# One transformer block on one core: the last 512 queries of attention in two jobs of 256, PSUM banks from one pool

## The chip, the core and the metric

One core of a Trainium2 chip runs the kernel. The metric is device time in microseconds (us), the median of several executions without a profiler. The profile pages come from one more execution with the hardware profiler on; its times are its own and are named as such. Engines in the profile: PE is TensorE (matmul), PEld its weight loads, DVE is VectorE, ACT is ScalarE, POOL is GpSimd, SP is SyncE, which issues the DMAs.

## The reference

One pre-norm transformer block on 2048 tokens of width 1024, in bf16. The attention has 32 heads of 32 columns, no mask. The feed-forward part (FFN) has 3584 hidden columns and a tanh GELU.

```
h  = x + softmax((ln(x) wq) (ln(x) wk)^T * 32**-0.5) (ln(x) wv) wo     # per head, heads joined
h2 = h + gelu(ln(h) w1 + b1) w2 + b2
```

The kernel gets `A_x`, `A_wqkv`, `A_wo`, `B_w1`, `B_b1`, `B_w2`, `B_b2` and writes `h2`.

## The kernel before

**A planner writes the order.** The kernel's Python describes every instruction as a `Task` with an engine, a cost in us, the buffers it reads and writes, a priority and a kind. `Graph.schedule` (L98) plays the tasks through by these costs and fixes the order of each engine's queue; `assign` adds the semaphore waits and `emit` writes the queues out. On the chip each engine then runs its queue strictly in that order, however long things take there. The costs are constants: a 512-column matmul pack 0.2225 us (`MM` and 0.003), an exp of 1024 columns 0.953 us (`c_act`), DMA 280 GB/s and 2.1 us latency, 0.1 us for a change of TensorE's tiling.

**What TensorE does next** is `pick_pe` (L913): a ready QK task always; else a PV task if five are waiting (`PV_FORCE`), if no background is ready, or after the last QK; else the oldest ready background task ("bg"). ScalarE, VectorE and SyncE take the ready task of lowest priority number, then the oldest.

**Attention.** The queries are cut in four chunks of 512. A head pair `p16` (16 of them) is worked on at a time; `g` is a group of two pairs, 128 columns. One round (`attention_round`, L687, `Att.qk`, L619) is one QK task: four matmuls with 32-row tiling at once, two key tiles of 128 by two heads, into four PSUM banks (L634). Two exp instructions on ScalarE follow (L643), each 128x1024 from two banks into a slot of the ring `PT`. There are three such two-bank units, banks 0 to 5. A PV task (`pv_unit`, L647) adds one key tile: two matmuls with V (L654) and two with a matrix of ones (L658), each on 32 columns of the array, all at once, into bank 6. A pair has 8 rounds, 16 exps and 16 PV tasks; then `finish` (L665) copies sums and outputs out of bank 6 on VectorE (L666, L668), and after the second pair of a group takes reciprocals (L673) and multiplies into `OT` (L680; in the very last group by quarters, L677). `load_q` fetches the group's queries from DRAM.

**Background.** While chunk `qc` is in attention, the work of chunk `qc - 1` runs between its rounds, in bank 7 alone: `wo` (L703, output projection, 8 accumulations of 8 matmuls, evicted into `hch` by L719), `ln2` (L723, layer norm per tile of 128 tokens on VectorE and GpSimd, eight transposes, L508, and their eviction into `hnT`, L512 or L514), `ffn1` (L735, 28 accumulations of 8, eviction with bias L748, then square, L754, scalar_tensor_tensor, L756, Tanh on ScalarE, L758, and L760 into `gT`) and `ffn2` (L763, for each half `j` of the output columns and each of four token tiles one bias matmul and 28 matmuls, evicted by L782). In the background every 128x128 by 512 matmul is issued as four matmuls on 32 columns each (`narrow`, L439), so that TensorE need not change its tiling between background and PV. Weights come in 512 KB tiles: `w1r` has four buffers, `w2r` seven. In the chunks before the last, `late_q` also projects later queries.

**Tail.** After the last attention, chunk 3's `wo`, `ln2`, `ffn1` and `ffn2` run alone, with full 128x128 matmuls (L443), eight banks in turn, buffers `R2` laid over the keys and values, and evictions of `ln2` and `ffn1` on ScalarE (L512, L751).

Of the kernel before, what the change touches and what calls it, by code (L numbers as in the profile page):

```python
# [27 lines left out]
class Task:  # L28
    __slots__ = ("eng", "fns", "occ", "lat", "deps", "prio", "kind", "mode", "left", "succ", "ready", "done",
                 "order", "inc", "flow", "value", "lane", "waits", "bytes", "hold")  # L30

    def __init__(self, eng, fns, occ, lat, prio, kind, mode):
        self.eng, self.fns, self.occ, self.lat = eng, fns, occ, lat
        self.prio, self.kind, self.mode = prio, kind, mode
        self.deps = set()
        self.succ = []
        self.left = 0
        self.ready = 0.0
        self.done = None
        self.order = None  # L40
        self.inc = False
        self.flow = None
        self.value = 0
        self.lane = None
        self.waits = ()
        self.bytes = 0
        self.hold = None


class Graph:  # L50
# [7 lines left out]
    def __init__(self, n_lanes):  # L58
        self.tasks = []
        self.regions = {}  # L60
        self.n_lanes = n_lanes

# [35 lines left out]
    def schedule(self, pick_pe, switch=0.1, dma_rate=280.0, dma_lat=2.1, dma_issue=0.06):  # L98
# [13 lines left out]

        def release(t):
            t.ready = max([d.done - (d.lat if d.eng == t.eng == E.PE else 0.0) for d in t.deps], default=0.0)
            heapq.heappush(upcoming[t.eng], (t.ready, num[t], t))
            heapq.heappush(events, t.ready)
# [5 lines left out]
        while n < total:  # L122
# [5 lines left out]
            for e in self.ENGS:  # L128
                while free[e] <= now + 1e-9:
# [18 lines left out]
                    rd.remove(t)  # L148
                    start = now
                    if e == E.PE:  # L150
# [19 lines left out]
                    heapq.heappush(events, free[e])  # L170
                    n += 1
# [113 lines left out]
def build_kernel(nc, A_x, A_wqkv, A_wo, B_w1, B_b1, B_w2, B_b2, out):  # L285
# [143 lines left out]
    def pe(fns, occ, reads=(), writes=(), kind="bg", mode="full", prio=0, after=()):  # L429
        return gr.add(E.PE, fns, occ, 0.16, reads, writes, prio, kind, mode, after)  # L430

    def mm(bank, lhsT, rhs, start, stop, reads, narrow, cols=(0, 512)):
# [3 lines left out]
        if narrow:  # L436
            fns = []
            for j in range(4):
                fns.append(lambda p, j=j: p.matmul(psum[32 * j:32 * j + 32, bank, c0:c1], lhsT[:, 32 * j:32 * j + 32], rhs,  # L439
                                                   start=start, stop=stop, tile_position=(0, 32 * j), skip_group_check=True))  # L440
            pe(fns, occ, reads=reads, writes=[B_ps[bank]], mode="col")
        else:
            pe(lambda p: p.matmul(psum[:, bank, c0:c1], lhsT, rhs, start=start, stop=stop),  # L443
               occ, reads=reads, writes=[B_ps[bank]], mode="full")
# [61 lines left out]
    def transposes(src_ap, B_src, bank, dst_ap, B_dst, evac, prio):  # L506
        for dc in range(DC):
            pe(lambda p, dc=dc: p.transpose(psb[:, bank, dc * P:(dc + 1) * P], src_ap[:, dc * P:(dc + 1) * P], ident[:]),  # L508
               0.064, reads=[B_src, B_ident], writes=[B_ps[bank]], prio=prio)
        src = psb[:, bank, :].rearrange("p (dc t) -> p dc t", dc=DC)  # L510
        if evac == "act":
            act(lambda a: a.activation(dst_ap, src, ACT.Copy), 1024, reads=[B_ps[bank]], writes=[B_dst], prio=-1)  # L512
        else:
            dve(lambda v: v.tensor_copy(dst_ap, src), c_dve_ps(1024), reads=[B_ps[bank]], writes=[B_dst])  # L514

# [19 lines left out]
    def proj(which, g, tc, bank, evac, direct=False):  # L535

        blk, c = divmod(which * D + g * P, 512)
        for dc in range(DC):
            mm(bank, Wall[:, blk, dc, c:c + P], xnT[:, tc, dc, :], dc == 0, dc == DC - 1,
# [3 lines left out]
        if evac == "act":  # L543
            act(lambda a: a.activation(stg[:, s, :], psum[:, bank, :], ACT.Copy), 512,
                reads=[B_ps[bank]], writes=[B_stg[s]], prio=-1)
        else:
            dve(lambda v: v.tensor_copy(stg[:, s, :], psum[:, bank, :]), c_dve_ps(512), reads=[B_ps[bank]], writes=[B_stg[s]])  # L547
# [28 lines left out]
    def late_q(R, qc, gs):  # L576

        dma(R.xq[:, :, :], xd[qc - 1], P * 8192, reads=[B_xd[qc - 1]], writes=[R.B_xq], prio=0)
        for g2 in range(gs // 2, G // 2):
            s = wblock(R, A_wqkv[:, 256 * g2:256 * g2 + 256], 0)  # L580
            for k in range(2):
                g = 2 * g2 + k
                for dc in range(DC):
                    mm(7, R.w1[:, s, dc, k * P:k * P + P], R.xq[:, dc, :], dc == 0, dc == DC - 1,
                       [R.B_w1[s], R.B_xq], True)
                o = R.next("os", R.nos)
                dve(lambda v, o=o: v.tensor_copy(R.ost[:, o, :], psum[:, 7, :]), c_dve_ps(512),
                    reads=[B_ps[7]], writes=[R.B_ost[o]])
                dma(qd[g, qc], R.ost[:, o, :], P * 1024, reads=[R.B_ost[o]], writes=[B_qd[g][qc]], prio=0)

    def proj_v(tt, q, bank, evac):

        blk, c = divmod(256 * q, 512)
        blk += 4
        for k in range(2):
            tc, t4 = divmod(tt + k, 4)
            for dc in range(DC):
                mm(bank, xnT[:, tc, dc, t4 * P:(t4 + 1) * P], Wall[:, blk, dc, c:c + 256], dc == 0, dc == DC - 1,
                   B_W[blk][c // P:c // P + 2] + [B_xnTt[tc][t4]], True, cols=(256 * k, 256 * k + 256))
        dst = V[:, tt:tt + 2, 256 * q:256 * q + 256]  # L600
        src = psum[:, bank, :].rearrange("p (t c) -> p t c", t=2)
        wr = [B_V[4 * (tt + k) + q] for k in range(2)]
        if evac == "act":
            act(lambda a: a.activation(dst, src, ACT.Copy), 512, reads=[B_ps[bank]], writes=wr, prio=-1)
        else:
            dve(lambda v: v.tensor_copy(dst, src), c_dve_ps(512), reads=[B_ps[bank]], writes=wr)  # L606


    class Att:
# [9 lines left out]
        def qk(self, qc, units):  # L619

            fns, banks, rd, us = [], [], [], []
            for p16, kt in units:
                tc, k4 = divmod(kt, 4)
                half, i = divmod(k4, 2)
# [5 lines left out]
                for j in range(2):  # L630
                    r0 = 64 * half + 32 * j

                    def fn(p, j=j, r0=r0, u=u, p16=p16, tc=tc, i=i, qs=qs, pr=pr):
                        return p.matmul(psum[:, 2 * u + j, :], KT2[r0:r0 + 32, p16, tc, i, :],  # L634
                                        QT2[r0:r0 + 32, qs, pr, :], start=True, stop=True, tile_position=(r0, 0))
                    fns.append(fn)
                banks += [B_ps[2 * u], B_ps[2 * u + 1]]
                rd += [B_KT[4 * p16 + tc][half], B_QTh[qs][half][pr]]
            pe(fns, 0.224, reads=rd, writes=banks, kind="qk", mode="row")
            for (p16, kt), u in zip(units, us):  # L640
# [4 lines left out]
                self.pv.append((qc, p16, kt, s))  # L645

        def pv_unit(self, bank, first, last):  # L647
            qc, p16, kt, s = self.pv[self.done]
            self.done += 1
            g, pr = divmod(p16, 2)  # L650
            fns = []
            for j in range(2):
                h = 2 * p16 + j
                fns.append(lambda p, j=j, h=h: p.matmul(  # L654
                    psum[32 * j:32 * j + 32, bank, :], V[:, kt, 32 * h:32 * h + 32], PT[:, s, j, :],
                    start=first, stop=last, tile_position=(0, 32 * j), skip_group_check=True))
            for j in range(2):
                fns.append(lambda p, j=j: p.matmul(  # L658
                    psum[64 + 32 * j:96 + 32 * j, bank, :], ones32[:, :], PT[:, s, j, :],
                    start=first, stop=last, tile_position=(0, 64 + 32 * j), skip_group_check=True))  # L660
            pe(fns, 0.224, reads=[B_PT[s], B_V[4 * kt + (p16 // 4)], B_ones], writes=[B_ps[bank]], kind="pv", mode="col")
            if last:
                self.finish(qc, g, pr, bank)

        def finish(self, qc, g, pr, bank):  # L665
            dve(lambda v: v.tensor_copy(Dsb[64 * pr:64 * pr + 64, :], psum[64:128, bank, :]), c_dve_ps(512),  # L666
                reads=[B_ps[bank]], writes=B_Dsb[pr], prio=-1)
            dve(lambda v: v.tensor_copy(Osb[64 * pr:64 * pr + 64, :], psum[0:64, bank, :]), c_dve_ps(512),  # L668
                reads=[B_ps[bank]], writes=[B_Osb[pr]], prio=-1)
            self.fin.add((qc, g, pr))  # L670
            if (qc, g, 1 - pr) in self.fin:
                for k in range(4):
                    dve(lambda v, k=k: v.reciprocal(Dsb[:, 128 * k:128 * k + 128], Dsb[:, 128 * k:128 * k + 128]), 0.93,  # L673
                        reads=[B_Dsb[0][k], B_Dsb[1][k]], writes=[B_Dsb[0][k], B_Dsb[1][k]], prio=1)
                    if qc == NCH - 1 and g == G - 1:
                        c = slice(128 * k, 128 * k + 128)
                        dve(lambda v, c=c: v.tensor_tensor(OT[:, qc % 2, g, c], Osb[:, c], Dsb[:, c], ALU.mult), c_dve(128),  # L677
                            reads=[B_Dsb[0][k], B_Dsb[1][k]] + B_Osb, writes=[B_OT[qc % 2][g][k]], prio=1)
                if not (qc == NCH - 1 and g == G - 1):
                    dve(lambda v: v.tensor_tensor(OT[:, qc % 2, g, :], Osb[:, :], Dsb[:, :], ALU.mult), c_dve(512),  # L680
                        reads=B_Dsb[0] + B_Dsb[1] + B_Osb, writes=B_OT[qc % 2][g], prio=1)
# [5 lines left out]
    def attention_round(qc, p16, r):  # L687
        tc, i = divmod(r, 2)
        att.qk(qc, [(p16, 4 * tc + i), (p16, 4 * tc + 2 + i)])
        while len(att.pv) - att.done > PV_LAG:  # L690
            att.pv_unit(6, att.done % 16 == 0, att.done % 16 == 15)

    def attention_flush():
        while len(att.pv) > att.done:
            att.pv_unit(6, att.done % 16 == 0, att.done % 16 == 15)
# [7 lines left out]
    def wo(R, qc, banks, RX):  # L703
        nb = 0
# [3 lines left out]
        for t4 in range(4):  # L708
            for j in range(2):
                s = ws[2 * j]  # L710
                bank = banks[nb % len(banks)]
                nb += 1
                tt = qc * 4 + t4
                for k, g in enumerate([7, 0, 1, 2, 3, 4, 5, 6] if len(banks) == 1 else range(G)):
                    mm(bank, OT[:, qc % 2, g, t4 * P:(t4 + 1) * P], R.w1[:, s:s + 2, g, :], k == 0, k == 7,
                       [B_OT[qc % 2][g][t4], R.B_w1[s], R.B_w1[s + 1]], len(banks) == 1)
# [290 lines left out]
```

## Time and profile before

| | us |
|---|---|
| median of three executions | 1203.92 (1203.0 to 1205.25) |
| profiled execution, its span | 1417.9 |
| ScalarE, 1024 exps (L643) | 989.2 busy, 1.025 each |
| VectorE, all | 673.2 busy |
| L439 `a_w2r,gT`, FFN2 in the background, 2688 matmuls | 241.9 |
| L439 `a_hnT,a_w1r`, FFN1 in the background, 2688 matmuls | 215.2 |
| L443 `a_hnT,b_w1r` and `a_w2r,gT`, FFN1 and FFN2 of the tail | 64.5 and 64.1 |
| last exp ends, last matmul starts | 1255.0, 1413.4 |

How to read it: the profiled execution took 1417.9 us from first to last instruction, while the executions without profiler took 1203.92 us in the median, 0.849 of it. The page's row of TensorE clock shows 0.7 nearly everywhere (0.749 in the mean). The clock of the executions without profiler is not recorded. A group's busy time is the union of its instructions, from start to a modelled end, so groups that overlap on TensorE add up to more than the engine's own busy time.

### The profile page before, as it was taken

How to read it: one execution, taken by the hardware profiler on the slowest of the kernel's cores; microseconds unless marked ns; L12 is line 12 of the kernel's file. 1: busy time of each engine (PE TensorE's matmuls, PEld its weight loads, DVE VectorE, ACT ScalarE, POOL GpSimd, SP SyncE). 2: the span in 40 equal slices, each digit the busy share in tenths (PEclk: the TensorE clock that was granted, in tenths of full speed). 3: DMA queues.
4: the chain of work that ended last, by engine and by line, in shares of the span. 5: the costliest groups of instructions: out<-in, count | busy, mean ns of one | idle time of the engine just before them, and what ended most of it. 6: DMA issues, size and time to landing. Idle time of an engine off the chain costs nothing.

```text
span 1417.9 us, 37847 instructions
## 1 busy us (share of the span) xinstructions
PE 1366.2 (96%) x17326; PEld 510.9 (36%) x17336; DVE 673.2 (47%) x1165; ACT 1085.3 (77%) x1189; POOL 37.9 (3%) x96
## 2 busy tenths in 40 slices
PE   8999999999999999999999999999999999978999
PEld 5544443433333333332333333333333333324333
DVE  7354444443546774223547762225677612245710
ACT  4778787878888888888888888888988888844500
POOL 2000000000100000000100000000000000001000
PEclk7777777777777777777777777777777777766777
DMA  6800000025343222303342230422323322202222
GB/s 165 224 2 13 28 13 14 13 72 156 101 122 101 76 69 72 124 16 98 107 124 71 83 98 16 124 71 63 107 73 98 102 66 85 87 0 75 74 93 71
DMA packets 165793, 112.29 MB, mean 79 GB/s; under 512 B 25345, under 2 KB 162817, under 8 KB 164866
## 3 DMA queue, kind: packets, MB, share of 16 engines
q1 hardware_dynamic: 165634, 109.87, 26.2%
q8 instruction: 136, 2.23, 0.7%
q14 instruction: 23, 0.19, 0.1%
HBM read 98.58 MB, written 11.27 MB: 77 GB/s over the span
## 4 chain that ended last, share of the span: by engine, by line
PE 91%; ACT 4%; DVE 3%; issue 1%; POOL 1%; DMA 0%; POOLq 0%; DVEq 0%
PE ps L439 48%; PE ps L654 17%; PE ps L634 12%; PE ps L443 10%; ACT PT L643 3%; PE ps L658 2%; PE ps L798 1%; ACT xnT L512 1%; DVE a_xh L748 1%; PE ps L508 1%; DVE V L606 0%; DVE stg L547 0%; DVE Osb L668 0%; DVE Dsb L666 0%; DMA a_w1r<-in_A_wqkv_dram 0%
## 5 line engine op out<-in xcount | busy, mean ns | idle before, releaser
L643 ACT ACTIVATE PT<-ps 128x1024 bf16<-128x1024 f32 x1024 | 989.2, 1025 | 180.5 <-PE ps L634 166.1
L654 PE MATMUL ps<-PT,V 128*32 128x512 bf16 x2048 | 383.4, 457 | 13.7 <-DVE V L606 6.2
L658 PE MATMUL ps<-PT,ones 128*32 128x512 bf16 x2048 | 384.8, 458 | 0.0
L439 PE MATMUL ps<-a_w2r,gT 128*32 128x512 bf16 x2688 | 241.9, 452 | 0.0
L634 PE MATMUL ps<-QT,KT 32*128 32x512 bf16 x2048 | 216.7, 414 | 7.4 <-ACT PT L643 7.3
L439 PE MATMUL ps<-a_hnT,a_w1r 128*32 128x512 bf16 x2688 | 215.2, 454 | 4.0 <-DVE a_xh L748 3.2
L654 PEld LDWEIGHTS ps<-PT,V 128*32 128x32 bf16 x2048 | 103.3, 104 | 143.9 <-issue 89.3
L634 PEld LDWEIGHTS ps<-QT,KT 32*128 32x128 bf16 x2048 | 51.5, 91 | 272.3 <-ACT PT L643 164.5
L439 PE MATMUL ps<-xnT,Wall 128*32 128x512 bf16 x1344 | 111.6, 453 | 7.0 <-ACT xnT L512 4.8
L439 PEld LDWEIGHTS ps<-a_w2r,gT 128*32 128x32 bf16 x2688 | 77.3, 109 | 112.0 <-issue 103.3
L673 DVE RECIPROCAL Dsb<-Dsb 128x128 f32<-128x128 f32 x128 | 115.1, 928 | 1.0
L439 PEld LDWEIGHTS ps<-a_hnT,a_w1r 128*32 128x32 bf16 x2688 | 70.6, 107 | 108.0 <-issue 71.4
L782 DVE SCALAR_TENSOR_TENSOR a_ost<-ps,hch 128x512 bf16<-128x512 f32 x24 | 16.6, 692 | 189.8 <-PE ps L439 189.7
L658 PEld LDWEIGHTS ps<-PT,ones 128*32 128x32 bf16 x2048 | 103.5, 104 | 6.6 <-issue 6.6
L748 DVE TENSOR_SCALAR a_xh<-ps,b1f 128x512 bf16<-128x512 f32 x84 | 63.1, 751 | 81.3 <-PE ps L439 80.2
L666 DVE COPY Dsb<-ps 64x512 f32<-64x512 f32 x64 | 44.4, 694 | 101.5 <-PE ps L658 100.1
L439 PE MATMUL ps<-Wall,xnT 128*32 128x256 bf16 x2048 | 83.8, 314 | 0.0
L547 DVE CAST stg<-ps 128x512 bf16<-128x512 f32 x40 | 27.5, 689 | 89.2 <-PE ps L439 89.2
L443 PE MATMUL ps<-a_hnT,b_w1r 128*128 128x512 bf16 x219 | 64.5, 470 | 2.1 <-ACT a_hnT L512 1.5
L439 PEld LDWEIGHTS ps<-Wall,xnT 128*32 128x32 bf16 x2048 | 57.6, 107 | 22.7 <-issue 11.3
L443 PE MATMUL ps<-a_w2r,gT 128*128 128x512 bf16 x219 | 64.1, 461 | 0.5
L439 PE MATMUL ps<-a_w1r,OT 128*32 128x512 bf16 x768 | 63.1, 453 | 0.8 <-DVE hch L719 0.5
(69 smaller groups left out, 875.5 us busy)
## 6 DMA issues: line engine op xcount, KB each, us to landing
a_w2r<-in_B_w_dram SPq DMA_DIRECT2D x56, 512.0 KB, 4.6
a_w1r<-in_B_w_dram SPq DMA_DIRECT2D x42, 512.0 KB, 3.9
a_w1r<-in_A_wo_dram SPq DMA_DIRECT2D x16, 512.0 KB, 4.7
QT<-q_scratch SPq DMA_DIRECT2D x60, 128.0 KB, 2.8
b_w1r<-in_B_w_dram SPq DMA_DIRECT2D x14, 512.0 KB, 3.8
a_w1r<-in_A_wqkv_dram SPq DMA_DIRECT2D x11, 512.0 KB, 5.1
xrb<-in_A_x_dram SPq DMA_DIRECT2D x16, 256.0 KB, 3.9
Wall<-in_A_wqkv_dram SPq DMA_DIRECT2D x16, 256.0 KB, 5.4
```

What stands on the lines that cost most here:

```text
L439: fns.append(lambda p, j=j: p.matmul(psum[32 * j:32 * j + 32, bank, c0:c1], lhsT[:, 32 * j:32 * j + 32], rhs, start=start, stop=stop, tile ...
L443: pe(lambda p: p.matmul(psum[:, bank, c0:c1], lhsT, rhs, start=start, stop=stop), occ, reads=reads, writes=[B_ps[bank]], mode="full")
L508: pe(lambda p, dc=dc: p.transpose(psb[:, bank, dc * P:(dc + 1) * P], src_ap[:, dc * P:(dc + 1) * P], ident[:]), 0.064, reads=[B_src, B_ide ...
L547: dve(lambda v: v.tensor_copy(stg[:, s, :], psum[:, bank, :]), c_dve_ps(512), reads=[B_ps[bank]], writes=[B_stg[s]])
L634: return p.matmul(psum[:, 2 * u + j, :], KT2[r0:r0 + 32, p16, tc, i, :], QT2[r0:r0 + 32, qs, pr, :], start=True, stop=True, tile_position= ...
L643: act(lambda a, u=u, s=s: a.activation(PT[:, s, :, :], psum[:, 2 * u:2 * u + 2, :], ACT.Exp, bias=0.0, scale=SCALE), 1024, reads=[B_ps[2 * ...
L654: fns.append(lambda p, j=j, h=h: p.matmul(psum[32 * j:32 * j + 32, bank, :], V[:, kt, 32 * h:32 * h + 32], PT[:, s, j, :], start=first, st ...
L658: fns.append(lambda p, j=j: p.matmul(psum[64 + 32 * j:96 + 32 * j, bank, :], ones32[:, :], PT[:, s, j, :], start=first, stop=last, tile_po ...
L666: dve(lambda v: v.tensor_copy(Dsb[64 * pr:64 * pr + 64, :], psum[64:128, bank, :]), c_dve_ps(512), reads=[B_ps[bank]], writes=B_Dsb[pr], p ...
L673: dve(lambda v, k=k: v.reciprocal(Dsb[:, 128 * k:128 * k + 128], Dsb[:, 128 * k:128 * k + 128]), 0.93, reads=[B_Dsb[0][k], B_Dsb[1][k]], w ...
L748: dve(lambda v, i=i, fc=fc, bank=bank: v.tensor_scalar(R.xh[:, i, :], psum[:, bank, :], b1f[:, fc:fc + 1], None, ALU.add), c_dve_ps(512), ...
L782: dve(lambda v, o=o, t4=t4, j=j, bank=bank: v.scalar_tensor_tensor(R.ost[:, o, :], psum[:, bank, :], 0.5, hch[:, t4, 512 * j:512 * j + 512 ...
```

## The change

- The list `jobs` replaces the loop over chunks: chunks 0 to 2 as before, then chunk 3 as two jobs, queries 0 to 255 and 256 to 511, each over all heads and keys. Beside the first runs the background of chunk 2, beside the second that of the first half (two token tiles), and the tail holds the second half alone.
- In a job of 256 queries one QK task has eight matmuls of 256 columns: each bank takes two key tiles side by side. The exp instructions keep their size. A PV task has eight matmuls of 256 columns, for two key tiles. A pair has 4 rounds; `finish` copies 256 columns. Each of the two jobs loads the queries.
- `wo`, `ln2`, `ffn1` and `ffn2` take token tiles or columns. For 256 queries, `ffn1` puts two of its 28 column blocks into one bank (matmuls of 256 columns), evicts them separately and runs the GELU steps on both at once. Every weight is loaded once more, since five jobs load what four did.
- Accumulations of the background are groups, numbered in program order. The planner opens them strictly in that order and gives each a bank from a pool when its first matmul is picked; the bank returns when its readers are done. The pool holds bank 7 from the start of the main attention, and the other seven join after their last use by the attention.
- An eviction of `ffn1` or `ln2` has an alternative on ScalarE. Once all exps are planned, it goes to the engine that has less planned work waiting.

```diff
 def release(t):
+    if t.alt is not None and late():
+        e2, fns2, occ2, lat2 = t.alt
+        if load[e2] + occ2 < load[t.eng] + t.occ:
+            t.eng, t.fns, t.occ, t.lat = e2, fns2, occ2, lat2
+    load[t.eng] += t.occ
...
+                    if e == E.PE and t.grp is not None and t.grp.bank is None:
+                        x = min(banks(now))
+                        pool.remove(x)
+                        t.grp.bank = x[1]
+                        state["next"] += 1
...
-def qk(self, qc, units):
+def qk(self, qc, units, q0=0, nq=512):
+    nk = 512 // nq
...
-    return p.matmul(psum[:, 2 * u + j, :], KT2[r0:r0 + 32, p16, tc, i, :],
-                    QT2[r0:r0 + 32, qs, pr, :], start=True, stop=True, tile_position=(r0, 0))
+    return p.matmul(psum[:, 2 * u + j, nq * k:nq * k + nq], KT2[r0:r0 + 32, p16, tc, i, :],
+                    QT2[r0:r0 + 32, qs, pr, q0:q0 + nq], start=True, stop=True, tile_position=(r0, 0))
...
+            fns = [f for _, f in sorted(fns, key=lambda x: x[0])]
+            pe(fns, 0.224 if nk == 1 else 0.23, reads=rd, writes=banks, kind="qk", mode="row")
...
-def wo(R, qc, banks, RX):
+def wo(R, qc, RX, narrow, t4s=range(4)):
...
+                gp = gr.group()
...
+            for f in range(0, 2, nk):
+                fcs = [2 * blk + f + k for k in range(nk)]
+                gp = gr.group()
+                i = R.next("gl", R.ngl)
+                for k, fc in enumerate(fcs):
+                    fo = (fc % 2) * P
+                    for dc in range(DC):
+                        mm(gp, R.w1[:, s, dc, fo:fo + P], R.hnT[:, dc, cols], dc == 0, dc == DC - 1,
+                           [R.B_w1[s]] + hn, narrow, cols=(nq * k, nq * k + nq))
...
+    jobs = [(0, 0, 512), (1, 0, 512), (2, 0, 512), (3, 0, 256), (3, 256, 256)]
+    for n in range(1, len(jobs)):
+        qc, q0, nq = jobs[n - 1]
+        t4s = range(q0 // P, (q0 + nq) // P)
+        if n == 1:
             late_q(R1, 1, 2)
-        wo(R1, qc - 1, [7], R1)
-        ln2(R1, qc - 1, [7], (lambda qc=qc: late_q(R1, qc + 1, 0)) if qc + 1 < NCH else None)
-        ffn1(R1, qc - 1, [7])
-        ffn2(R1, qc - 1, [7])
-        attention_chunk(qc)
+        wo(R1, qc, R1, True, t4s)
+        ln2(R1, (lambda n=n: late_q(R1, n + 1, 0)) if n < 3 else None, t4s)
+        ffn1(R1, True, slice(q0, q0 + nq))
+        ffn2(R1, qc, True, t4s)
+        attention_chunk(*jobs[n])
         attention_flush()
...
+    for b in range(7):
+        gr.join(b, B_ps[b].w + B_ps[b].r)
...
+            if t.grp is not None and t.grp.bank is None and (not free or t.grp.n != state["next"]):
+                continue
```

## The prediction

> **What bounds the kernel now.** I read the page first: busy time by engine, the granted clock, the chain that ended last.
>
> ```profile
> span 1417.9 us, 37847 instructions
> PE 1366.2 (96%) x17326; PEld 510.9 (36%) x17336; DVE 673.2 (47%) x1165; ACT 1085.3 (77%) x1189; POOL 37.9 (3%) x96
> PEclk7777777777777777777777777777777777766777
> PE 91%; ACT 4%; DVE 3%; issue 1%; POOL 1%; DMA 0%; POOLq 0%; DVEq 0%
> ```
>
> TensorE is busy 96% of the span, is 91% of the chain, and runs at 0.75 of its clock. A change that only moves matmuls gains what TensorE idles now, no more. So I looked for its idle time around the last chunk: a table by stage. Columns: busy time of PE, PEld, DVE, ACT and POOL, each with its count, then clock, DMA share, GB/s.
>
> ```profile
> 960.00:1011.00 51.00, 46.86 (x592) 15.84 (x588) 30.47 (x51) 45.65 (x49) 6.21 (x16) 0.75 0.29 82
> 1011.00:1115.00 104.00, 102.52 (x1352) 35.64 (x1348) 75.47 (x124) 90.62 (x106) 0.00 (x0) 0.75 0.31 88
> 1115.00:1233.00 118.00, 117.75 (x1560) 39.62 (x1558) 33.46 (x47) 99.62 (x105) 0.00 (x0) 0.75 0.28 85
> 1233.00:1256.00 23.00, 18.92 (x164) 4.55 (x157) 2.66 (x4) 21.04 (x23) 0.00 (x0) 0.68 0.02 6
> 1256.00:1272.00 16.00, 15.37 (x57) 5.76 (x55) 11.66 (x20) 0.00 (x0) 0.00 (x0) 0.75 0.01 1
> 1272.00:1284.00 12.00, 3.96 (x32) 3.30 (x34) 6.86 (x19) 3.98 (x4) 6.38 (x16) 0.57 0.00 1
> 1284.00:1349.00 65.00, 64.34 (x220) 25.65 (x224) 45.46 (x80) 32.02 (x53) 0.00 (x0) 0.73 0.28 81
> 1349.00:1415.00 66.00, 65.44 (x228) 25.88 (x231) 7.61 (x12) 1.84 (x3) 0.00 (x0) 0.75 0.26 86
> ```
>
> The first three rows are the last chunk's attention with chunk 2's background beside it: output projection (wo) and layer norm (ln2), then FFN1, then FFN2. In FFN1 and FFN2 TensorE has 1.7 us free out of 222. Only after 1233 is there room (18.92 of 23). Then comes the tail alone: wo, a hole of 12 us while ln2 runs on VectorE and GpSimd, FFN1, FFN2.
>
> The timeline of TensorE fixes where the background ends:
>
> ```profile
> 1232.31 0.76 PE L439 MATMUL ps<-a_w2r,gT 128*32 128x512 bf16 x8
> 1245.02 0.39 PE L634 MATMUL ps<-QT,KT 32*128 32x512 bf16 x4 [0.50 <-ACT PT L643]
> 1246.85 0.42 PE L634 MATMUL ps<-QT,KT 32*128 32x512 bf16 x4 [0.47 <-ACT PT L643]
> ```
>
> Chunk 2's last FFN2 matmul starts before 1233. By the same view ten QK rounds follow (1233.27 to 1252.35). Without background a round lasts 1.83 us (1245.02 to 1246.85) and waits for ScalarE.
>
> **The change, part by part.** Units first. I call four narrow matmuls that start together, or one full one, a pack. FFN2 of the tail is 232 packs (224 and 8 of bias) in the 66 us from 1349 to 1415: 0.2845 us each. A round's own work is one QK and two PV packs, 0.85, plus two changes of tiling. The timeline shows 0.415 from a column pack to QK and 0.351 from QK back, against 0.2845: 0.20 together. So a round without background leaves 1.83 - 1.05 = 0.78 us, 2.7 packs.
>
> *Where the moved work lands.* The two jobs together have the same 128 rounds. Chunk 2's background keeps its place in TensorE's order and keeps its 520 packs, so it still ends some ten rounds before the end, now inside the second job. The first half's background (wo 32 packs, FFN1 112, FFN2 116) queues behind it, in strict order of groups. In ten rounds only its wo fits: chunk 2's wo took 31.2 us for 64 packs (965.8 to 997.0), so 32 take 15.6, from 1233 to about 1249. FFN1 and FFN2 of the first half therefore still run after the attention, as narrow packs, and the second half's wo, ln2, FFN1 and FFN2 behind them. So the change mostly cuts the tail in two rather than hiding it.
>
> *The tail before*, from the last PV pack at 1256.8: wo 14.5, hole 12.8 (to 1284.1), FFN1 64.5, FFN2 66.4, last eviction and store 2.9: 161.1.
>
> *The tail after*, term by term:
> - Hole until FFN1 of the first half. From the last wo pack to FFN1, chunk 2 took 14.2 (997.0 to 1011.2) for four tiles. Two tiles, ending at 1249, give between 7 and 14, so FFN1 starts at 1256 to 1263. Bounds 0 to 8; I take 4.
> - FFN1, 112 x 0.2845 = 31.9, as 224 packs of 256 columns. The V projection has such packs (groups by shape): 83.8 us for 512 of them, 0.164 each, against 0.142 for half a pack. But that busy time counts ends; start to start the timeline mostly shows 0.138. I take 0.142.
> - FFN2, 116 x 0.2845 = 33.0.
> - Waits for w2 tiles: seven buffers, now freed and refilled within one token tile's 8 us instead of three times that. Seven tiles at the fastest rate of the trace, 329 GB/s (1380 to 1385), take 11.2 us plus latency. Bounds 0 to 3 for each half; I take 1.5.
> - wo of the second half, 32 x 0.2845 = 9.1.
> - Second hole. At least the last tile's chain: 0.69 hch, 1.28 statistics, 0.2, about 2.2 on GpSimd, 0.55, 1.0 transposes, 1.0 eviction: 7. At most the 12.8 of today. I take 9.
> - Slow clock behind the holes: 0.73 instead of 0.75 over 65 us is 1.7 today. For two holes I take 2.7.
> - FFN1 31.9, FFN2 33.0, tile wait 1.5, end 2.9.
>
> Sum 160.5, against 161.1: nothing gained. Wo moved into the rounds pays for the second hole, and not more.
>
> *What is added in the attention.* Every head pair now hands over PSUM bank 6 twice per 512 queries, 16 handovers more. ScalarE waited for PV 12.9 us in all (waits), over 64 handovers: 0.2 each, 3.2 (bounds 0 and twice that). Wo beside the last rounds: 1.0. QK and PV of 256 columns double the instructions and weight loads; PV is nearest to the V projection's rows and costs nothing. QK packs back to back on the same rows occur nowhere. Bounds: 0, or a weight load of 0.091 uncovered in each of 128 rounds, 11.6. I take 0, since ScalarE sets many of those rounds. QT is loaded 16 times more (128 KB, 2.8 us), ahead of use and behind free slots; the 16.8 MB of weights loaded once more come at a mean of 79 GB/s today. Both nothing, unless SyncE's queue holds them back; that is in the tile waits.
>
> *Shared evictions.* The tail's ScalarE did 28 evictions and its FFN1 ran at PE 64.34 of 65, so moving some to VectorE, already busy 45.46, releases nothing. The pool is one bank during the attention, as before. Nothing for both; that cover goes if VectorE takes most evictions: 14 pairs x (1.8 + 0.8) is 36 us, 4 over the matmuls.
>
> Total: 161.1 becomes 160.5 + 4.2, so 1417.9 becomes **1421.5**. The profiled execution was slower than the three timed runs: 1203.92 / 1417.9 = 0.849. If all scales alike, 1207. If plain runs have the full clock, packs shrink by a quarter (35.8 us off the old tail, 34.7 off the new), while holes and waits stay and tile waits double (+3): -0.6 + 1.1 + 3.0 + 4.2 = +7.7, or 1211.6. The trace does not tell which; I take the middle, **1209**.
>
> A rule that speaks against the change: the Trainium skill, "TensorE: Matmul & The Clock Gate", section "What's actually happening", says that an idle window of about 3.4 us halves the array's clock, and knows only full and half clock. The trace has 0.75 for over a millisecond, so here the measurement decides, and it has 0.57 in the 12 us hole. By the page each hole costs about one window at half rate, an estimate of 1.7 us of work: 3.4 for two, 0.7 more than my term.
>
> **Rivals.**
> - *The second job has room after all (faster).* If chunk 2's background leaves more rounds to the first half, each hides 0.78 us of tail. For it: 0.78 us free per round without background. Against: TensorE busy 117.75 of 118 where the work would have to go. Eighteen rounds more give 18 x 0.78 x 0.849 = 12 us: **1197**. It decides from eleven rounds more (11 x 0.66 = 7.3, more than 5.1 and the 0.2%).
> - *Half packs cost (slower).* The uncovered QK weight load, 11.6, and narrow FFN1 at 0.164 instead of 0.142, 224 x 0.022 = 4.9: 16.5 x 0.849 = 14 more, **1223**. For it: no row shows QK packs back to back. Against: weight loads lie beside matmuls everywhere (PEld 36%).
> - *It doesn't do what it says:* the halves change nothing measurable. That is my forecast with smaller holes, and its share of "same".
>
> **How the numbers follow.** Forecast 0.56 (own range 1200 to 1217), faster rival 0.25, slower rival 0.19. Lowest bounds of all terms: 160.5 - 4 - 2 - 3 - 1, so -10.6 x 0.849 = 1195; highest: +10.9 for holes, waits and clock, 6 handovers, 1, 11.6: 29.5 x 0.849 = 1229. Beside the rivals, 8 in 10 is 1193 to 1225. About 0.2% (2.4 us) is what a measurement of this kernel can tell from no change. Faster: 0.25 + 0.04 = 0.29. Same: 0.17. Slower: 0.35 + 0.19 = 0.54.
>
> **What would show it.** Right: narrow FFN1 and FFN2 packs (256 columns in FFN1) after the last exp; two holes of 4 to 10 us with a low clock; chunk 2's last FFN2 pack about ten rounds before the last QK. Wrong: narrow FFN packs of the first half between QK rounds (room); rounds above 1.83 us without background (half packs); matmuls of FFN1 waiting for w1 tiles (transfers).

## The result and the profile after

The changed kernel takes **1208.93 us** (median of four, 1208.04 to 1210.17), the kernel before 1203.93 beside it: a ratio of 1.0043 [1.0028, 1.0057], 5.0 us slower. The page of the changed kernel, the lines that answer to those shown of before:

```profile
span 1208.3 us, 43762 instructions
PE 1130.7 (94%) x20212; PEld 517.9 (43%) x20212; DVE 683.4 (57%) x1219; ACT 1060.0 (88%) x1201; POOL 37.6 (3%) x96
PEclk9999999999999999999999999999999999999989
PE 69%; ACT 13%; DVE 10%; DMA 4%; issue 2%; SPq 1%; POOL 0%; POOLq 0%; DVEq 0%
```

The clock is nearly full. The profiled execution of before that the prediction worked from had been granted 0.75, an exception: before, profiled again (run e1 below), has a clock of 0.989 and this page:

```profile
span 1201.3 us, 37847 instructions
PE 1129.4 (94%) x17326; PEld 465.1 (39%) x17336; DVE 668.7 (56%) x1165; ACT 1060.0 (88%) x1189; POOL 37.9 (3%) x96
```

So from here on 1201.3 and 1208.3 are compared, not 1417.9. TensorE is as busy as before to within 1.3 us, so 5.7 of the 7.0 us between the spans are idle time of TensorE. The table by stage says where. The changed kernel, from the last QK rounds to the end (length; busy PE, PEld, DVE, ACT, POOL with counts; clock; DMA share; GB/s):

```profile
1050.00:1069.00 19.00, 17.65 (x408) 8.72 (x400) 12.25 (x24) 18.95 (x22) 2.16 (x7) 1.00 0.47 127
1069.00:1073.40 4.40, 1.22 (x24) 0.57 (x16) 3.17 (x7) 1.68 (x2) 0.89 (x2) 1.00 0.22 53
1073.40:1107.10 33.70, 28.81 (x896) 26.67 (x900) 25.11 (x50) 13.61 (x26) 0.00 (x0) 0.90 0.69 192
1107.10:1135.80 28.70, 25.87 (x472) 12.79 (x463) 6.48 (x11) 2.33 (x4) 0.00 (x0) 1.00 0.89 275
1135.80:1142.80 7.00, 7.00 (x36) 3.05 (x32) 4.27 (x7) 0.00 (x0) 0.00 (x0) 1.00 0.42 143
1142.80:1150.30 7.50, 2.18 (x18) 1.56 (x18) 3.38 (x8) 2.05 (x2) 3.05 (x8) 0.67 0.00 1
1150.30:1179.40 29.10, 27.56 (x225) 22.89 (x226) 21.20 (x39) 17.75 (x36) 0.00 (x0) 0.91 0.67 181
1179.40:1205.40 26.00, 25.52 (x118) 11.08 (x115) 5.86 (x10) 2.27 (x5) 0.00 (x0) 1.00 0.59 192
```

Row by row: the last ten rounds, with the first half's wo; the first hole; the first half's FFN1 and FFN2; the second half's wo; the second hole; its FFN1 and FFN2. The same table of before, profiled again: last rounds, wo, hole, FFN1, FFN2.

```profile
1051.00:1073.00 22.00, 17.53 (x161) 4.51 (x157) 2.84 (x5) 21.07 (x23) 0.00 (x0) 0.84 0.05 17
1073.00:1084.40 11.40, 11.40 (x56) 4.96 (x55) 10.27 (x18) 0.00 (x0) 0.00 (x0) 1.00 0.01 1
1084.40:1097.50 13.10, 4.18 (x34) 3.31 (x35) 7.75 (x21) 3.99 (x4) 6.38 (x16) 0.66 0.00 1
1097.50:1148.00 50.50, 50.29 (x219) 22.46 (x223) 44.16 (x79) 32.09 (x53) 0.00 (x0) 0.95 0.36 104
1148.00:1198.40 50.40, 50.01 (x228) 22.60 (x231) 8.23 (x14) 1.84 (x3) 0.00 (x0) 1.00 0.35 112
```

One hole of 13.1 has become two of 4.4 and 7.5, and wo of 11.4 has become 7.0 outside the rounds. That would be a gain of about 6. But the two FFN1 take 62.8 instead of 50.5, and the two FFN2 54.7 instead of 50.4. In the first half's FFN1 TensorE is busy 28.81 of 33.70. The cause is not in the attention: chunk 3's 256 exps take 256.3 us from the start of the first to that of the last before, and 255.4 after.

The timeline of TensorE in the changed kernel shows what the first half found (start, length, engine, line, tile, shape, count; L511 is the narrow matmul, L719 QK):

```profile
1049.56 0.39 PE L511 MATMUL ps<-a_w2r,gT 128*32 128x512 bf16 x4
...
1050.10 0.40 PE L719 MATMUL ps<-QT,KT 32*128 32x256 bf16 x8
1050.82 1.05 PE L511 MATMUL ps<-a_w1r,OT 128*32 128x512 bf16 x16 [0.32 <-DVE a_ost L890]
```

Chunk 2's last FFN2 pack runs at 1049.6, ten QK rounds follow (1050.10 to 1067.23), and only wo of the first half fits between them, with the transposes of one token tile.

### The profile page after: what moved, and what is told of

Read it like the earlier page. It is cut to its first block, busy times and chain, and to the rows that moved or that the text cites. A ratio compares the mean times of both kernels' runs of the same rounds, so it can differ in the third digit from the quotient of the medians.

```text
span 1208.3 us, 43762 instructions
## 1 busy us (share of the span) xinstructions
PE 1130.7 (94%) x20212; PEld 517.9 (43%) x20212; DVE 683.4 (57%) x1219; ACT 1060.0 (88%) x1201; POOL 37.6 (3%) x96
## 3 DMA queue, kind: packets, MB, share of 16 engines
q8 instruction: 158, 2.59, 0.9%
## 4 chain that ended last, share of the span: by engine, by line
PE 69%; ACT 13%; DVE 10%; DMA 4%; issue 2%; SPq 1%; POOL 0%; POOLq 0%; DVEq 0%
PE ps L511 42%; ACT PT L729 12%; PE ps L745 12%; PE ps L719 10%; PE ps L515 4%; DVE a_xh L864 3%; DMA a_w2r<-in_B_w_dram 2%; ACT xnT L587 1%; DVE a_uu L837 1%; DVE Dsb L771 1%; DVE gT L843 1%; DMA q_scratch<-stg 1%; DVE Osb L762 1%; SPq L532 1%; DVE Dsb L760 1%
## 5 line engine op out<-in xcount | busy, mean ns | idle before, releaser
L729 ACT ACTIVATE PT<-ps 128x1024 bf16<-128x1024 f32 x1024 | 967.3, 1035 | 29.6 <-PE ps L719 16.7
L745 PE MATMUL ps<-PT,V 128*32 128x512 bf16 (+1 forms) x2560 | 315.8, 338 | 13.0 <-DVE V L689 5.3
L749 PE MATMUL ps<-PT,ones 128*32 128x512 bf16 (+1 forms) x2560 | 315.8, 338 | 0.0
L511 PE MATMUL ps<-a_w2r,gT 128*32 128x512 bf16 x3136 | 224.6, 381 | 2.8 <-DMA a_w2r<-in_B_w_dram 2.8
L511 PE MATMUL ps<-a_hnT,a_w1r 128*32 128x512 bf16 (+1 forms) x3584 | 203.2, 359 | 17.2 <-DVE a_xh L864 10.4
L719 PE MATMUL ps<-QT,KT 32*128 32x512 bf16 (+1 forms) x2560 | 202.6, 340 | 12.8 <-ACT PT L729 9.1
L719 PEld LDWEIGHTS ps<-QT,KT 32*128 32x128 bf16 x2560 | 54.1, 91 | 209.6 <-ACT PT L729 164.9
L511 PEld LDWEIGHTS ps<-a_hnT,a_w1r 128*32 128x32 bf16 x3584 | 87.7, 98 | 99.6 <-issue 28.5
L511 PEld LDWEIGHTS ps<-a_w2r,gT 128*32 128x32 bf16 x3136 | 82.0, 96 | 88.9 <-issue 31.0
L511 PE MATMUL ps<-xnT,Wall 128*32 128x512 bf16 x1344 | 91.3, 381 | 8.9 <-ACT xnT L587 5.5
L760 DVE COPY Dsb<-ps 64x512 f32<-64x512 f32 (+1 forms) x80 | 47.0, 587 | 90.4 <-PE ps L749 88.6
L864 DVE TENSOR_SCALAR a_xh<-ps,b1f 128x512 bf16<-128x512 f32 (+1 forms) x97 | 69.0, 711 | 40.0 <-PE ps L511 37.2
L839 ACT ACTIVATE a_th<-a_uu 128x512 f32<-128x512 bf16 x98 | 62.4, 638 | 11.3 <-DVE a_uu L837 10.8
L511 PE MATMUL ps<-Wall,xnT 128*32 128x256 bf16 x2048 | 68.3, 273 | 0.1
L843 DVE SCALAR_TENSOR_TENSOR gT<-a_th,a_xh 128x512 bf16<-128x512 f32 x98 | 66.3, 677 | 3.6 <-ACT a_th L839 3.1
L837 DVE SCALAR_TENSOR_TENSOR a_uu<-a_sq,a_xh 128x512 bf16<-128x512 bf16 x98 | 66.7, 682 | 1.9
L511 PE MATMUL ps<-a_w1r,OT 128*32 128x512 bf16 x896 | 61.3, 381 | 2.2 <-DVE hch L821 1.0
```

Source lines behind the costliest of these rows:

```text
L719: return p.matmul(psum[:, 2 * u + j, nq * k:nq * k + nq], KT2[r0:r0 + 32, p16, tc, i, :], QT2[r0:r0 + 32, qs, pr, q0:q0 + nq], start=True, ...
L729: act(lambda a, u=u, s=s: a.activation(PT[:, s, :, :], psum[:, 2 * u:2 * u + 2, :], ACT.Exp, bias=0.0, scale=SCALE), 1024, reads=[B_ps[2 * ...
L745: fns.append(lambda p, j=j, h=h, kt=kt, cols=cols, st=st, sp=sp: p.matmul(psum[32 * j:32 * j + 32, bank, 0:nq], V[:, kt, 32 * h:32 * h + 3 ...
L749: fns.append(lambda p, j=j, cols=cols, st=st, sp=sp: p.matmul(psum[64 + 32 * j:96 + 32 * j, bank, 0:nq], ones32[:, :], PT[:, s, j, cols], ...
L760: dve(lambda v: v.tensor_copy(Dsb[64 * pr:64 * pr + 64, 0:nq], psum[64:128, bank, 0:nq]), c_dve_ps(nq), reads=[B_ps[bank]], writes=B_Dsb[p ...
L837: dve(lambda v: v.scalar_tensor_tensor(R.uu[:, i, :], R.sq[:, i, :], C2, R.xh[:, i, :], ALU.add, ALU.mult), c_dve(512), reads=[R.B_sq[i], ...
```

## The experiments

Each ratio is against the kernel before, timed beside it. My theory behind the first ones: the moved work finds no room, the tail is cut in two, and what the cut adds outweighs the hole it removes.

**e1: the kernel before, unchanged.** 

> The kernel before, unchanged, for a profile that may have the clock of the changed kernel's profile (0.993). Theory (the tail is cut in two, nothing is hidden): at a clock near 1.0 the span is 1200 to 1206, chunk 2's last background matmul starts at 1044 to 1050, about ten QK rounds follow it, and from there to the end it takes 150 to 155 us against 158.5 in the changed kernel (1049.8 to 1208.3). Rival (the attention itself got slower): the last background matmul starts at 1040 to 1044, and the rest takes as long as in the changed kernel, within 1 us.

Span 1201.3, clock 0.989, last background pack at 1050.6 (0.6 past my range), 150.7 us before the end where the changed kernel takes 158.7: the theory held. So the order on the engines at full clock is the one that the prediction read at 0.75, and its terms can be compared at full clock.

**e2: the pool and the shared evictions, without the two jobs.**

```diff
-    jobs = [(0, 0, 512), (1, 0, 512), (2, 0, 512), (3, 0, 256), (3, 256, 256)]
+    jobs = [(0, 0, 512), (1, 0, 512), (2, 0, 512), (3, 0, 512)]
```

> The changed kernel with chunk 3 again as one job of 512 queries: what is left is the pool of banks and the shared evictions of the tail. Theory (the split costs the 5 us): 1202 to 1206, same as the kernel before. Rival (pool or shared evictions cost them): 1207 to 1210, as the changed kernel.

1204.03, ratio 1.0001 [0.9991, 1.0010]. The whole loss comes from the two jobs. Pool and sharing without them are worth nothing that can be measured.

**e3: all tail evictions on ScalarE.**

```diff
-                if load[e2] + occ2 < load[t.eng] + t.occ:
+                if True:
```

> The changed kernel, but every eviction of the tail that may go to ScalarE goes there, as in the tail of the kernel before. Theory (TensorE's own rate and gaps set the two FFN1 parts, 33.7 and 29.1 us): 1207 to 1211. Rival (the evictions on VectorE hold FFN1 up): 1200 to 1205.

1210.44, ratio 1.0054 [1.0042, 1.0067], whose interval overlaps that of the change. The first half's FFN1 still takes 32.8. VectorE's share of the evictions is not what makes it slow.

**e4: full 128x128 matmuls in the first half's FFN1 and FFN2**, which run after the attention anyway.

```diff
-        ffn1(R1, True, slice(q0, q0 + nq))
-        ffn2(R1, qc, True, t4s)
+        ffn1(R1, nq == 512, slice(q0, q0 + nq))
+        ffn2(R1, qc, nq == 512, t4s)
```

> The changed kernel with full 128x128 matmuls in FFN1 and FFN2 of the first half, which run after the attention anyway: a quarter of the instructions for the same columns. Theory (narrow packs of 256 columns are limited by the feeding of instructions: 0.139 us a pack where the V projection's take less, and 4.8 us of gaps with no releaser but issue): FFN1 of the first half takes 25 to 28 us instead of 33.7, FFN2 26 to 28 instead of 28.7, in all 1200 to 1203. Rival (weight tiles or VectorE set FFN1): 33 us stay, 1207 to 1210.

1203.82, ratio 0.9998 [0.9987, 1.0009]: the loss is gone, though time and FFN1 end just above my ranges. FFN1 falls from 33.7 to 28.2, FFN2 from 28.7 to 26.2. The timeline of TensorE in the changed kernel shows what was between the narrow packs:

```profile
1073.41 8.73 PE L511 MATMUL ps<-a_hnT,a_w1r 128*32 128x256 bf16 x251 [1.11 <-ACT a_hnT L590]
1082.62 3.68 PE L511 MATMUL ps<-a_hnT,a_w1r 128*32 128x256 bf16 x128 [0.48 <-issue]
1087.74 7.43 PE L511 MATMUL ps<-a_hnT,a_w1r 128*32 128x256 bf16 x255 [1.44 <-issue]
1097.22 8.83 PE L511 MATMUL ps<-a_hnT,a_w1r 128*32 128x256 bf16 x254 [2.05 <-issue]
1106.89 0.40 PE L511 MATMUL ps<-a_hnT,a_w1r 128*32 128x256 bf16 x8 [0.84 <-issue]
```

Four gaps, 4.8 us, put down to "issue": no semaphore released TensorE there. Over the 8.9 us after the longest gap (2.05) the clock is 0.81, which costs a further 1.7 us. With full matmuls (L515) in e4 the breaks are short and have a named cause, a weight tile:

```profile
1077.27 14.50 PE L515 MATMUL ps<-a_hnT,a_w1r 128*128 128x256 bf16 x112 [1.12 <-ACT a_hnT L590]
1092.17 7.22 PE L515 MATMUL ps<-a_hnT,a_w1r 128*128 128x256 bf16 x64 [0.41 <-DMA a_w1r<-in_B_w_dram]
1100.05 5.41 PE L515 MATMUL ps<-a_hnT,a_w1r 128*128 128x256 bf16 x48 [0.66 <-DMA a_w1r<-in_B_w_dram]
```

**e5: fill the second hole.** The second half's wo is moved ahead of the first half's FFN2, with a buffer `hnT` of its own; ln2 and the second column half of that FFN2 follow.

```diff
-        ffn2(R1, qc, True, t4s)
+        if nq == 512:
+            ffn2(R1, qc, True, t4s)
...
+    R2.hnT, R2.B_hnT = sb(att_area, "b_hnT", [P, DC, 512], BF, 1, 4)
-    R2.hnT, R2.B_hnT = R1.hnT, R1.B_hnT
...
     wo(R1, qc, R2, False, t4s)
+    ffn2(R1, qc, True, range(0, 2), (0,))
     ln2(R2, None, t4s)
+    ffn2(R1, qc, True, range(0, 2), (1,))
```

> The changed kernel with another order behind the attention: the second half's output projection ahead of the first half's FFN2, its layer norm and transposes between the two column halves of that FFN2, and a hidden-state buffer of its own for them (four x buffers instead of eight make the room). Theory (the strict order puts the second layer norm in the open: 7.5 us of hole and some slow clock behind it): 1199 to 1203, 6 to 10 under the changed kernel's 1208.9. Rival (the second hole hides waits for weight tiles that come out anyway): 1206 to 1209.

1209.60, ratio 1.0066 [1.0054, 1.0078]: my theory fell. The hole is gone, but FFN1's gaps are 6.1 us in e5, and its timeline has new waits:

```profile
1114.53 8.51 PE L515 MATMUL ps<-a_w1r,OT 128*128 128x512 bf16 x32 [4.51 <-DMA a_w1r<-in_A_wo_dram]
...
1160.44 8.98 PE L515 MATMUL ps<-b_hnT,b_w1r 128*128 128x256 bf16 x80 [3.18 <-DMA b_w1r<-in_B_w_dram]
```

The wo weights go into the ring `a_w1r`, whose buffers the first half's FFN1 reads until the moment wo now wants to start.

**e6: e5 and e4 together.** 

> The order of the run before this one, and full matmuls in FFN1 and FFN2 of the first half. Theory: both gains add, 5 and 6 to 10 under 1208.9, so 1194 to 1198, and faster than the kernel before. Rival (weight transfers set the tail: two sets of 16.8 MB in some 130 us): 1200 to 1204.

1206.28, ratio 1.0033 [1.0020, 1.0046]: both ranges missed. FFN1 takes 27.6 us here instead of e5's 33.4, and wo's wait for its weights grows to 6.11.

**e7 and e8: is it room that is missing?** Chunk 2's FFN2 leaves out its second column half, 116 packs, in the kernel before (e7) and in the changed one (e8).

```diff
-        for j in range(2):
+        for j in range(1 if qc == 2 else 2):
```

> The kernel before, but chunk 2's FFN2 computes only the first 512 output columns: 116 packs and a quarter million stores of the background are left out, so some 26 rounds at the end of the attention have no background. Theory (these rounds wait for ScalarE anyway): 1200 to 1204, as with the work. Rival (TensorE sets these rounds): 1180 to 1195.

> The changed kernel with the same part of chunk 2's FFN2 left out: now the second job has room. Theory (room is what the change lacks): the first half's output projection, layer norm and most of FFN1 go between rounds, 1175 to 1190, clearly faster than the kernel before with the same part left out. Rival (the split costs its 5 us whatever the room): 1204 to 1209.

e7: 1205.03, ratio 1.0016 [1.0007, 1.0026], 1 us above my range; less work and no gain. e8: 1179.06, ratio 0.9808 [0.9795, 0.9821]. The last rounds, one row of the table by stage each, e7 first:

```profile
1005.00:1075.00 70.00, 54.82 (x491) 12.66 (x484) 15.36 (x21) 69.48 (x76) 0.00 (x0) 0.73 0.06 19
```

```profile
1001.00:1079.00 78.00, 69.15 (x1968) 45.12 (x1960) 58.53 (x114) 76.69 (x88) 3.06 (x8) 1.00 0.56 157
```

In e7 ScalarE sets the rounds (69.48 of 70) and TensorE idles. In e8 the same gaps hold the first half's wo and FFN1, and ln2 runs beside them. Given room, the two jobs do hide the work: 2.1% of 1203, 25 us. In the whole kernel chunk 2's background has taken that room. The kernel before at full clock (e1), beside chunk 2's FFN1 and FFN2:

```profile
863.60:956.20 92.60, 87.59 (x1388) 32.16 (x1388) 77.48 (x127) 90.39 (x109) 0.00 (x0) 1.00 0.35 98
958.20:1050.60 92.40, 91.92 (x1500) 35.38 (x1496) 28.63 (x41) 91.90 (x99) 0.00 (x0) 1.00 0.33 104
```

TensorE has 5.5 us free in 185.0 and ScalarE 2.7. The prediction, at a clock of 0.75, saw only TensorE full.

**e9: own weight slots for the early wo.** As e6, and wo's weights go into `b_w1r`, the second FFN1's into `a_w1r`.

```diff
-    wo(R1, qc, R2, False, t4s)
+    wo(R2, qc, R2, False, t4s)
+    R2.w1, R2.B_w1, R2.cnt["w1"] = R1.w1, R1.B_w1, R1.cnt["w1"]
```

> As the run e6_wo_first_full, but the second half's output projection takes its weights into the four b_w1r buffers (free since the keys are done) and the second FFN1 into a_w1r, the other way round. Theory (the reordering lost its gain to one new wait: 6.1 us for the wo tiles, which found no free buffer until the first half's FFN1 was through): that wait goes, 1199 to 1203. Rival (the DMA engines as a whole set the tail, 270 to 330 GB/s in places): the wait comes back at another tile, 1204 to 1207.

**1195.65** (1193.53 to 1198.08), ratio 0.9945 [0.9932, 0.9958]: faster than both kernels and below both ranges. e9's timeline:

```profile
1093.79 7.17 PE L515 MATMUL ps<-a_hnT,a_w1r 128*128 128x256 bf16 x64 [0.78 <-DMA a_w1r<-in_B_w_dram]
1100.79 7.07 PE L515 MATMUL ps<-b_w1r,OT 128*128 128x512 bf16 x32
...
1144.11 19.41 PE L515 MATMUL ps<-b_hnT,a_w1r 128*128 128x256 bf16 x160 [3.31 <-DMA a_w1r<-in_B_w_dram]
```

FFN1 runs into wo without a break (no bracket behind the second line), and wo takes 7.07 us instead of e6's 8.97, where the clock behind the wait was 0.78. A wait of 3.31 for a weight tile is left. From the last exp's start to the end e9 takes 122.9, before 130.3.

**e10: are narrow matmuls slow by themselves?** Without the two jobs (e2), the tail's FFN1 and FFN2 narrow, 512 columns.

```diff
-    ffn1(R2, False, slice(q0, q0 + nq))
-    ffn2(R2, qc, False, t4s)
+    ffn1(R2, True, slice(q0, q0 + nq))
+    ffn2(R2, qc, True, t4s)
```

> The run e2_no_split with FFN1 and FFN2 of the whole tail as narrow packs of 512 columns instead of full matmuls: four times the instructions, each pack 0.214 us. Theory (only packs of 256 columns outrun the feeding of instructions): 1202 to 1207, as e2. Rival (narrow packs cost by themselves): FFN1 and FFN2 of the tail grow by 10% or more, 1212 or more.

1204.37, ratio 1.0015 [1.0005, 1.0026]. No: FFN1's 896 narrow matmuls run in 49.91 us without a break, where full ones took 50.5 (e1). FFN2 takes 53.1 instead of 50.4, of which 2.3 are waits for w2 tiles.

```profile
1095.17 49.91 PE L511 MATMUL ps<-a_hnT,b_w1r 128*32 128x512 bf16 x896 [1.11 <-ACT a_hnT L590]
```

**e11: is it the weights' traffic?** The first half's FFN1 loads only the first 4 of its 14 weight blocks and uses them again.

```diff
-            s = wblock(R, B_w1[:, 256 * blk:256 * blk + 256])
+            s = wblock(R, B_w1[:, 256 * blk:256 * blk + 256]) if blk < 4 or not (narrow and nq == 256) else blk % 4
```

> The changed kernel, but the first half's FFN1 loads only four of its fourteen weight blocks and computes with these again and again (its numbers are left wrong; matmuls and evictions are all there): 5.2 MB less traffic while it runs. Theory (the feeding of instructions alone holds the narrow packs of 256 columns back): the gaps stay, FFN1 32 to 34 us, 1207 to 1209. Rival (the weights' traffic makes the gaps, by itself or by delaying the instructions' own transfers): FFN1 24 to 29 us, 1200 to 1205.

1202.15, ratio 1.0001 [0.9990, 1.0012]. The same narrow instructions, with 47 GB/s in this stretch instead of 192, take 26.7 us instead of 33.7, and one gap of 0.43 is left:

```profile
1074.61 26.19 PE L511 MATMUL ps<-a_hnT,a_w1r 128*32 128x256 bf16 x891 [1.11 <-ACT a_hnT L590]
1101.22 0.38 PE L511 MATMUL ps<-a_hnT,a_w1r 128*32 128x256 bf16 x5 [0.43 <-issue]
```

My theory fell and the rival held. So neither the narrow form (e10) nor its 256 columns alone (e11) makes the gaps: it takes narrow 256-column packs and heavy traffic together. FFN2 of the first half agrees: narrow with 512 columns, at 275 GB/s, it has no gap put down to "issue".

What TensorE lacks in a gap is its own instructions. The changed kernel's page has one queue for them, with 158 packets and 2.59 MB:

```profile
q8 instruction: 158, 2.59, 0.9%
```

That is 16384 bytes a packet, and over TensorE's 40424 matmuls and weight loads 64 bytes each: 256 instructions, or 128 narrow matmuls with their weight loads, to a packet. The gaps come after 251, 379, 634 and 888 matmuls, at most 8 short of a multiple of 128. The trace also records when each packet starts and ends (the views print only the sums). Packets end at 1081.19, 1086.41, 1095.58 and 1105.49, and matmuls go on at 1082.62, 1087.74, 1097.22 and 1106.89. All 22 gaps in the narrow FFN1 of the changed kernel, e3, e5 and e12 end 1.3 to 1.6 us after the end of such a packet.

Traffic does not make the packets longer (0.9 to 1.1 us, in e11 0.9 to 1.3) but later. Counted from the first matmul of the 128 before, they start after 1.2 to 3.2 us, in e11 after 0.3 to 0.8; e11's sixth starts after 1.5 and makes its one gap. Such a block of 128 matmuls lasts 3.5 us in e11. With 1.1 for the packet and 1.4 behind it, a start within about a microsecond is in time (an estimate from these numbers). A block of 512 columns lasts twice as long (7.1 in e10). Where a packet is held up before it starts, no run shows.

**e12: e9 with narrow matmuls in the first half.** 

> The order and the buffers of the run e9_own_slots, but with the first half's FFN1 and FFN2 as narrow packs, as in the changed kernel: it prices the second hole by itself. Theory (hole and narrow packs are two separate costs, 8 and 5 us): 1199 to 1203, and no wait of over 2 us for wo tiles. Rival (the two overlap, and only both together help): 1205 to 1209.

1204.40 (1200.16 to 1209.46), ratio 1.0014 [0.9998, 1.0029]: between the two ranges. Against the changed kernel, 0.0029 or 3.5 us for the second hole alone; against e9, 0.0069 or 8.3 us for the narrow form, where e4 gave 0.0045 or 5.4. Both repairs together (e9 against the change) give 0.0098 or 11.8 us, and one by one 3.5 and 5.4. With some 2 us of uncertainty in each of these, it is not shown that they are worth more together. The traces speak against it: from the last exp's start to the end e12 takes 128.1, only 5.2 more than e9, and the rest of what separates the two traces lies before that exp, where their work is the same (it starts at 1072.7 in e12, 1068.8 in e9). FFN1 of e12 has six gaps, 4.4 us in all.

## Why the prediction was right, and which of its terms were not

It forecast 1209, slower, and 1208.93 was measured. Its steps, at full clock (its packs times 0.75), against the profile:

| step | predicted | measured |
|---|---|---|
| rounds left for the first half, and what fits | ten, wo alone | ten, wo alone |
| old tail, last PV to end | 125.3 | 128.2 |
| new tail, last PV to end | 128.8 | 138.5 |
| first hole | 4 | 3.6 |
| FFN1, first half | 23.9 | 33.7 |
| FFN2, first half, with tile waits | 27.8 | 28.7 |
| wo, second half | 6.8 | 7.0 |
| second hole | 9 | 7.5 |
| FFN1, second half | 23.9 | 29.1 |
| slow clock behind the holes | 2.7 | 1.7 and 2.6, inside the two FFN1 rows |
| FFN2, second half, with tile waits | 27.8 | 26.0 |
| extras in the attention | 4.2 | -1 to 0 |

- **The mechanism was right: the tail is cut in two and nothing is gained.** "In ten rounds only its wo fits", "cuts the tail in two rather than hiding it": the trace has both, e2 puts the loss on the two jobs, and e8 shows that room is what lacks. (The view behind the ten rounds of before has eleven QK starts; the changed kernel has ten.) Without FFN1's gaps the change is even: 0.9998 in e4, 1.0001 in e11.
- **The term mis-sized is FFN1 of the first half**, 9.8 short. I asked of its packs only how long one takes. The gaps (4.8) have no row in the profile of before, because narrow 256-column packs and fast weight traffic never meet there. Slow clock is 3.4 more: 0.81 over 8.8 us behind the hole, which the sum had in a term of its own, and 0.81 over 8.9 behind the longest gap. The remaining 1.6 I have not broken down. My list of wrong signs named matmuls that wait for w1 tiles; the waits here are for instructions, held up while w1 comes in (e11).
- **That the number was hit is luck.** The sum at full clock has 3.5 more in the tail and 4.2 in the attention, and the forecast is the middle between its 1211.6 and the 1207 of the slow clock. Measured are 9.4 more from the last exp's start to the end (130.3 to 139.7) and nothing in the attention: two errors with opposite signs. The medians are only 5.0 apart. In the trace of the changed kernel the last exp starts at 1068.6, in e1 at 1071.0; in e3, whose work is the same up to there, it starts at 1073.1 and the rest takes 136.9. So one trace does not place the last few microseconds.
- **The 3.2 for handovers of bank 6 rested on a misread row.** ScalarE's 12.9 us of waits for PV are ten waits, not one for each of 64 handovers, and six of them lie in the first chunk (the row below). The changed kernel waits 9.3 us in eight, as the kernel before does in e1. Wo beside the last rounds, priced at 1.0, cost nothing either.
- **The clock.** I took the middle of 1207 and 1211.6. The record has the clock of the timed executions after all: 0.986 to 0.997, and 0.973 to 0.982 in e7. So the arm for full clock, 1211.6, was the one that applied.
- **The slower rival** put its price on QK packs of 256 columns, 11.6; that is nothing. Its other part, narrow FFN1 packs that cost more than half a pack, is what happened, for a reason it did not have.
- **The faster rival** needed eleven rounds more. There were none; e8 gives it what it asked for, and then it is worth 25 us.
- **"Nothing" for shared evictions and for the pool** held (e2, e3).

ScalarE's waits for PV in the profile of before, from 0 to 340 us (time in all, times, longest):

```profile
ACT PT L643 <- PE ps L658: 11.6, 6, 2.5
```

The rule of the Trainium skill that I weighed, "TensorE: Matmul & The Clock Gate", section "What's actually happening", knows half and full clock. Behind the holes the traces agree in kind: 0.67 in the second hole, 0.91 over the 29.1 us behind it. The 1.7 us a hole that I estimated from that section stands against 1.7 behind the first hole and 2.6 behind the second. The 0.75 for over a millisecond in one execution of before has no place in it, and no run here had it again.

## What to carry to other kernels

Work that is moved under another stage needs idle time there: read it from the stage, after the work that already lies in it, and test it by leaving some of that out. When the bound is an order written ahead, a filled hole can come back as a wait for a buffer that the order frees late: look for who still reads the buffers that the moved step loads into (e6 against e9, 10.6 us). And when matmuls get shorter while transfers get denser, look in the timeline for gaps that no semaphore explains, and count the instructions between them; an operation that must no longer share TensorE with the attention should take the form with the fewest instructions.

## What was not expected of the hardware

- One execution of the kernel before was granted 0.75 of the clock throughout (1417.9 us); the same kernel profiled again had 0.989 (1201.3).
- Narrow packs of 256 columns lose 4.4 to 6.1 us of FFN1's 31.7 to 33.7 to gaps of "issue" while weights come in (four runs); the same packs with a quarter of the traffic lose 0.43. Each gap ends 1.3 to 1.6 us after a packet of 256 instructions has ended.
- A gap of 2.05 us was followed by 8.9 us at a clock of 0.81.
- QK in packs of 256 columns, twice as many matmuls and weight loads back to back on the same rows, costs nothing here: 255.4 us for 256 exps against 256.3, and 0.33 us from its start to the PV pack behind it (1067.23 in the changed kernel) against 0.32 (1051.15 in e1).
